# adaLN block with sliding-window attention and a gated spatial MLP: a second norm written as seven blocks of 64, its modulation in 64-row products, and a new order of all queues

## The chip, the cores and the metric

The kernel runs on one core of a Trainium2 chip. The core has five engines, each with its own queue of instructions that it works in order: TensorE (PE, matrix products; PEld is its loading of weights), VectorE (DVE), ScalarE (ACT), GpSimd (POOL) and SyncE (SP), which here only issues DMA transfers. The metric is the time of one execution on the device in microseconds; each kernel is run several times and the median is compared.

## What is computed

The input x has 2048 rows (tokens) of 448 columns. A row c of 448 gives, through silu and a product with w_mod, six rows of 448 (sa, ca, ga, sb, cb, gb). Everything is bfloat16.

```python
mod = (silu(c) @ w_mod).reshape(6, 448)          # sa, ca, ga, sb, cb, gb
h = layernorm(x) * (1 + ca) + sa
x = x + ga * attention(h, wqkv, wo)               # 16 heads of 28, causal, window of 256 rows
h = layernorm(x) * (1 + cb) + sb
z = gelu(h @ w_in)                                # 2 x 896 columns
z1, z2 = z[:, :896], layernorm(z[:, 896:])
g = w_sp @ z2 + b_sp                              # 2048 x 2048: mixes the rows
out = x + gb * ((z1 * g) @ w_out)
```

## The kernel before

**Stages.** x is held as 16 tiles of 128 rows. (1) To some 27 us: loads, the first modulation (sa, ca), the first norm and Q, K, V of the first block of four tiles. While nothing else can run, TensorE works filler products (L564). (2) To some 110 us: attention, tile by tile (scores L925, L955 and L966, exponential on ACT L911, mask on DVE L974, probabilities times V L1002, output product L1028), with Q, K and V of the next blocks of 512 rows in between (L762, L796, L820, L840). (3) To some 155 us: the gMLP's input products (L1122 for z2, L1143 for z1). (4) To some 261 us: the spatial mixing, 28 groups of 16 products (L1167), each followed by an addition on DVE (L1171) and a product on POOL (L1174). (5) Between and behind these, the output products (L1186), the last addition (L1196) and the stores.

**What sets the order.** The program creates some 1,175 operations, numbered as they are created, with the engines that each may run on and the operations that it depends on. A long string, PLAN, then has one word for each: a letter for the engine (p PE, a ACT, d DVE, t POOL, s SP), the operation's number, and the buffer slots it takes. The words stand in one global order; each engine works its own words in that order, and the waits on semaphores follow from the dependences. Priorities and costs that are also written in the code are not read when PLAN is there. So an engine can be held by a word whose input is late, and all its later words wait behind it.

**The loads.** SyncE issues, in the plan of before and in this order: x of tiles 0 and 1 (L408), two halves of wmodA, half of wk (L404), x of tiles 2 and 3, half of wq, x of tiles 4 to 7 (L398), x of 8 to 11, wv, wmodB (L393; the columns of w_mod for ga, sb, cb, gb, 1,568 KB), the four transposes of the first norm of tiles 4 to 7 (L465, from xn to hT), x of tiles 12 to 15, wo, and then transposes of later tiles among five loads of w_in (L432, L434). ACT issues c and the other halves of wmodA, wk and wq; its silu of c stands behind them.

**w_in** is 448 x 1792 and lies in four chunks of the 128 partitions: three of 128 rows, and one of the last 64 rows, which is loaded twice, once into each half of the partitions. This is so because the products L1122 and L1143 are made in pairs of 64 rows each: one uses partitions 0 to 63, the other 64 to 127, and the two of a pair belong to different outputs. by_halves (L1091) says which 64-row chunk of which output goes with which: chunks 0 to 5 are the halves of the three full chunks, and chunk 6 is the doubled one.

**The norm** (L635) computes (x - mean) * rstd into xn, on DVE (L643) or as x * rstd + (-mean * rstd) on POOL or DVE (L650). For the second norm, 448 columns are written as they are, and a second instruction (L655, L656) copies the last 64 of them again behind, so that after the transpose the last 64 rows of hT stand in both halves of the partitions. That is 16 copies of 128 x 64.

**The second modulation** (sb, cb) has to lie in the same layout. mod_cols (L526) makes it as 32 products with 112 x 128 weights from wmodB. For the last 64 columns, doubled, it takes wmodE, which two copies (twice, L581) fill from wmodB. mod_out (L553, L554) copies the result to modT. The rows ga and gb are made by 8 products of L593, from wmodB too.

Of the kernel before, what the change touches and what calls it, by code (L numbers as in the profile page):

```python
# [5 lines left out]
BF16 = mybir.dt.bfloat16  # L6
# [6 lines left out]
d24 d22 p50.1 p59.3 p51.2 p58.0 p60.1 p62.0 a0 a3 a5 a7 a9 d23 d25 d26 d27 p40.1 p68.2 p74.3 p64.1 p52.0 p67.2  # L13
p53.3 p76.0 p49.3 p70.0 s1 s2 s4 d113 s6 s10 s8 a41 p45.0 p46 p47.1 p48 p73.2 p75.1 p63.2 t30 t31 t32 t35 t36
t33 d111 d114 t34 d112 t115 t37 a103 t29 t105 t38 d117.3 d116.2 p125.7 d86 d85 p128.0 p78.0 a129 a130 d106
d126 d127 d120 d121 d118 d119 a107 p83.1 p80.0 p81.1 p79.2 p77.0 p55.3 p72.2 p71.0 s12 d183 d181 p65.1 t104
p54.0 p149.1 p84.2 p140.5 p141 p150 a151 p82.1 p57.2 a142 t109 t110 t108 p137.7 p138 a139 p66.2 t122 d124.2
d123.0 p134.3 p131.6 p69.3 p56.0 p146.0 p147 p61.2 a132 d177 d184 d135 a136 s13 d243 d179 d178 d182 d180 t28
t185 t191 t187 t189 d245 d44 d241 d186.3 s11 p143.7 p370.0 a133 p164.1 p171.6 p172 d244 p165 d166 a148 p152.0
p144 d145 d173 d247 p153 d154 a371.0 p376.0 p155.1 p156 d157 a42 a377.4 p394.0 a395.1 a396 a170 t39 d380 d372  # L20
d246 d167 d374 p158.7 p159 a160 s15 p93.1 p94 d95 d248 d87 d88 d242 d397 p96.0 p97 d98 d378 s193 t188.1 s194
t190.2 s195 t192.0 s196 d197 d200 p401.0 a402.5 p174.1 p175 a176 p161.7 p162 p373.0 p89.0 p90 d91 d198 d92
a403 a43 p421.0 a422.6.0 t249 t253 d404 t251 t199 p375 p379 p381 d406 d382 d399 t252.2 d163 p217.0 p218 a219
a169 p210.1 p211 d212 p429.0 a430.0 p201.0 p202 a203 d168 p204.1 p205 a206 s14 d309 d383.2 p398.0 p400 p448.0
a449.2.1 s16 d426 s831 s258 t254.1 s259 d250.0 d255 d425 d432 d311 s384 s257 t256.3 s260 t100 t99 t261 t102
t262 t264 p226.0 p423.0 a424 p207.1 p227 p405 p208 d228 d305 p407 d408 d409.1 d306 s410 d101 d310 d431 a209
# [224 lines left out]
def bass_adaLN_cond__sliding_block__mixer_gmlp__prompt_kernel(  # L251
# [16 lines left out]
    DC = 4  # L268
# [366 lines left out]
    def norm(slot, t, to, h, deps, prio, share, twice=False):  # L635
# [17 lines left out]
        if not twice:  # L653
            return op
# [614 lines left out]
```

## Time and profile before

| | us |
|---|---|
| runs of the kernel | 277.11, 276.43, 281.8; median 277.11 |
| the profiled execution | 277.96 |
| its span in the profile | 276.2 |
| granted clock of TensorE, mean | 0.993 |
| TensorE busy | 268.5 |
| DVE, ACT, POOL busy | 163.7, 121.5, 118.1 |

The profile is that of one execution. Its page gives the busy time of each engine, the span in 40 slices, the DMA queues, the chain of work that ended last, and groups of instructions by source line. Other views of the same trace give single instructions with what they waited for, the chain in order of time, and stretches of time with each engine's busy time. Matmuls are pipelined, so an instruction's length on PE (say 0.35 us) is longer than the distance to the next one.

### The profile page before, as it was taken

To read this page: it belongs to the slowest core of one execution; us is meant where nothing else is said; L and a number is where in the kernel's file an instruction comes from. 1 tells how busy PE (TensorE), PEld (TensorE's weight loads), DVE (VectorE), ACT (ScalarE), POOL (GpSimd) and SP (SyncE) were. 2 spreads that over 40 slices of the span, in tenths; PEclk is the share of its full clock that TensorE was granted. 3 is DMA by queue.
4 is the path that set the end of the run, shared out by engine and by line. 5 is a ranking of instruction groups with operands and counts; after the bars stand their busy time and mean duration, and the time that the engine had idled before them with its cause. 6 is when DMAs were issued, how large, how long until landed. Compare 5 with 4: busy or idle time off the path is not lost.

```text
span 276.2 us, 8403 instructions
## 1 busy us (share of the span) xinstructions
PE 268.5 (97%) x3751; PEld 155.1 (56%) x3751; DVE 163.7 (59%) x365; ACT 121.5 (44%) x142; POOL 118.1 (43%) x160
## 2 busy tenths in 40 slices
PE   7999998999999899999999999999999999999995
PEld 5976686678677676544444444444444444454552
DVE  3799999979899989939789301221212022153143
ACT  2599998899899689476766500000000000000000
POOL 7565467626574231498258003254453023062320
PEclk9999999999999799999999999999999999999999
DMA  7999744845442533658499996000000000001013
GB/s 206 316 221 189 96 101 114 107 96 110 114 63 61 107 60 61 176 114 141 97 155 191 213 182 135 0 0 0 2 0 0 0 2 0 33 17 63 0 39 116
DMA packets 67301, 25.54 MB, mean 92 GB/s; under 512 B 58497, under 2 KB 66178, under 8 KB 67266
## 3 DMA queue, kind: packets, MB, share of 16 engines
q1 hardware_dynamic: 66304, 24.21, 43.8%
q10 hardware_dynamic: 962, 0.80, 1.1%
q8 instruction: 29, 0.48, 0.8%
q14 instruction: 6, 0.05, 0.1%
HBM read 9.01 MB, written 1.84 MB: 39 GB/s over the span
## 4 chain that ended last, share of the span: by engine, by line
PE 78%; DVE 13%; DMA 4%; POOL 1%; SPq 1%; issue 1%; DVEq 0%
PE ps L1167 35%; PE ps L1122 8%; PE ps L1143 8%; PE ps L1186 8%; PE ps L1002 5%; DVE PT L974 4%; PE ps L1028 4%; PE ps L955 3%; DMA x_sb<-in_A_x_dram 3%; PE ps L820 3%; PE ps L762 2%; DVE st_all L628 2%; PE ps L840 2%; DMA hT<-xn 2%; DVE o_sb L1018 1%
## 5 line engine op out<-in xcount | busy, mean ns | idle before, releaser
L1174 POOL TENSOR_TENSOR z1T<-tmpg,z1T 128x512 bf16<-128x512 bf16 x28 | 32.0, 1153 | 77.2 <-DVE tmpg L1171 77.2
L1171 DVE TENSOR_TENSOR tmpg<-ps,bsp_bc 128x512 bf16<-128x512 f32 x28 | 19.0, 689 | 76.0 <-PE ps L1167 64.7
L911 ACT ACTIVATE PW<-ps 128x2048 bf16<-128x2048 f32 (+1 forms) x42 | 59.9, 1451 | 6.1 <-PE ps L955 4.5
L1167 PE MATMUL ps<-wspB,z 128*128 128x512 bf16 x224 | 50.1, 379 | 0.0
L1167 PE MATMUL ps<-wspA,z 128*128 128x512 bf16 x224 | 49.5, 379 | 0.0
L632 POOL TENSOR_TENSOR rs_all<-mv_all,neghalf 128x1 f32<-128x1 f32 (+2 forms) x37 | 24.1, 672 | 34.3 <-DVE mv_all L630 34.3
L974 DVE TENSOR_TENSOR PT<-PW,mask 128x1024 bf16<-128x1024 bf16 x56 | 38.0, 702 | 0.2
L1167 PEld LDWEIGHTS ps<-wspA,z 128*128 128x128 bf16 x224 | 21.8, 98 | 26.6 <-issue 0.4
L1167 PEld LDWEIGHTS ps<-wspB,z 128*128 128x128 bf16 x224 | 21.9, 98 | 26.2
L1002 PE MATMUL ps<-Vaug,PT 128*128 128x32 bf16 x496 | 23.3, 177 | 1.4 <-DVE o_sb L1018 1.4
L1002 PEld LDWEIGHTS ps<-Vaug,PT 128*128 128x128 bf16 x496 | 21.4, 96 | 4.3 <-DVE o_sb L1018 2.2
L1122 PE MATMUL ps<-w_in,hT 64*128 64x448 bf16 x224 | 22.0, 350 | 0.0
L1186 PE MATMUL ps<-w_out_g,z1T 128*128 128x448 bf16 (+2 forms) x119 | 22.0, 342 | 0.0
L1143 PE MATMUL ps<-hT,w_in 64*128 64x512 bf16 x196 | 22.0, 376 | 0.0
L628 DVE BATCH_NORM_STATS2 st_all<-z 128x6 f32<-128x448 bf16 x32 | 18.4, 606 | 5.8 <-ACT z L1129 5.8
L628 DVE BATCH_NORM_STATS2 st_all<-x_sb 128x6 f32<-128x448 bf16 x32 | 19.4, 615 | 2.9 <-DMA x_sb<-in_A_x_dram 2.7
L1002 PE MATMUL ps<-Vaug,PW 128*128 128x32 bf16 x224 | 19.7, 177 | 0.0
L820 PE MATMUL ps<-hT,WQK 112*128 112x128 bf16 x256 | 17.9, 223 | 1.6 <-DVE KT L833 1.1
L1151 ACT ACTIVATE z1T<-ps 128x512 bf16<-128x512 f32 x28 | 14.6, 603 | 9.1 <-PE ps L1143 9.1
L1196 DVE TENSOR_TENSOR fin<-ps,x_sb 128x448 bf16<-128x448 f32 (+2 forms) x17 | 9.8, 595 | 14.7 <-PE ps L1186 9.9
L1002 PEld LDWEIGHTS ps<-Vaug,PW 128*128 128x128 bf16 x224 | 17.6, 96 | 1.1
L1129 ACT ACTIVATE z<-ps 128x896 bf16<-128x896 f32 x16 | 13.9, 913 | 7.9 <-PE ps L1122 5.4
(105 smaller groups left out, 354.1 us busy)
## 6 DMA issues: line engine op xcount, KB each, us to landing
out_dram<-fin SPq DMA_DIRECT2D x15, 112.0 KB, 1.7
wmodB<-in_w_mod_dram SPq DMA_DIRECT2D x1, 1568.0 KB, 15.0
x_sb<-in_A_x_dram SPq DMA_DIRECT2D x3, 448.0 KB, 8.0
w_in<-in_B_w_in_dram SPq DMA_DIRECT2D x3, 448.0 KB, 4.5
w_out_g<-in_B_w_out_dram SPq DMA_DIRECT2D x1, 784.0 KB, 4.7
bsp_bc<-in_B_b_sp_dram SPq DMA_DIRECT2D x1, 512.0 KB, 5.1
x_sb<-in_A_x_dram SPq DMA_DIRECT2D x2, 224.0 KB, 4.8
hT<-xn SPq DMA_TRANSPOSE x28, 3.2
```

Source lines behind the costliest of these rows:

```text
L628: st = [dve(0.62, lambda e, t=t, o=12 - 6 * (n - ci), s=s: e.bn_stats(st_all[:, slot, t, o:o + 6], s()), deps(t), prio) for ci, s in enume ...
L632: return pool(0.4 + 0.15 * len(tiles), lambda e: e.tensor_tensor(rs_all[:, slot, a:b], mv_all[:, slot, a:b, 1], neghalf[:, 0:b - a], ALU.pow),
L820: km = lambda g, kc, start, stop, h=h, t=t: lambda e: e.matmul(ps[:, h.slot[0], g * 128:(g + 1) * 128], lhsT=WQK[0:CP, kc, 16 + 4 * g:20 + ...
L911: ex = act(xdur, lambda e, out_ap=out_ap, in_ap=in_ap: e.activation(out_ap(), in_ap(), ACT.Exp, scale=SCALE), [s] + list(after), v - 8.0 + ...
L974: return lock_d(0.68, lambda e: e.tensor_tensor(cols(hp.slot[0] * 2048 + 1024 * k, [[256, 4], [128, 2], [1, 128]]), cols(at_w() + pad + at ...
L1002: fns.append(lambda e, hp=hp, hO=hO, hi=hi, bi=bi, kb=kb, hd=hd, nb=nb, a=at[hi][bi], p_of=p_of: e.matmul(ps[:, hO.slot[0], 32 * hd:32 * h ...
L1122: return lambda e, kc, p0, start, stop: e.matmul(ps[:, hs[t % 2].slot[hf], 0:D], lhsT=hT[p0:p0 + 64, kc, t * 128:(t + 1) * 128], rhs=w_in[ ...
L1143: return lambda e, kc, p0, start, stop: e.matmul(ps[:, hs[b // 2].slot[b % 2], :], lhsT=w_in[p0:p0 + 64, kc, ft * 128:(ft + 1) * 128], rhs ...
L1167: m = pe(16 * MMS, [lambda e, h=h, si=si, ft=ft, tb=tb: e.matmul(ps[:, h.slot[0], :], lhsT=z2[:, si, ft * 128:(ft + 1) * 128], rhs=(wspA i ...
L1171: a = dve(0.7, lambda e, h=h, ht=ht, tb=tb: e.tensor_tensor(tmpg[:, ht.slot[0], :], ps[:, h.slot[0], :], bsp_bc[:, tb * 512:(tb + 1) * 512 ...
L1174: u = pool(1.16, lambda e, ht=ht, ft=ft, tb=tb: e.tensor_tensor(z1T[tb][:, ft, :], tmpg[:, ht.slot[0], :], z1T[tb][:, ft, :], ALU.mult), [ ...
L1186: return [lambda e, ft=ft: e.matmul(ps[:, h.slot[0], 0:hi - lo], lhsT=z1T[t // 4][:, ft, (t % 4) * 128:(t % 4 + 1) * 128], rhs=w_out_g[:, ...
```

## The change

The change makes the layout of the second norm uniform. The 448 columns are covered by eight blocks of 64, numbered by half u (0, 1) and chunk c (0 to 3): the block starts at column 192 u + 64 c. Columns 192 to 255 are thus in two blocks, u = 0, c = 3 and u = 1, c = 0; as columns these are seven different blocks.

- The norm of the second kind reads x through a four-dimensional pattern (halves) and writes 512 columns in one instruction; the 16 copies are gone.
- w_in is loaded to match in four loads of 64 partitions and two chunks each (448 KB each, 1,792 KB in all as before) instead of five.
- The second modulation is made as 64 products with 112 x 64 weights, each for one half of the output's partitions (tile_position (0, 64 u)), straight from wmodB; wmodE and its two copies are gone.
- by_halves pairs chunk n of the lower half with chunk n or n + 1 of the upper half.
- PLAN is new, with 1,156 words. Its numbers are counted anew, too, since fewer operations are created.

The diff without PLAN:

```diff
     wmodB, _, wmodB_bytes = alloc("wmodB", [128, DC, 4 * D], BF16, at=wspA_off + NT * HS)
-    wmodE, _, wmodE_bytes = alloc("wmodE", [128, DC, 2, 128], BF16, at=wspA_off + NT * HS + wmodB_bytes)
...
-    t_win_l = [load("d_win%d" % ch, "sp", 0.46, lambda e, ch=ch: e.dma_start(w_in[:, ch, :], B_w_in[ch * 128:(ch + 1) * 128, :]), (), -46.0 + 0.1 * ch)
-               for ch in range(3)]
-    t_win_l += [load("d_winh%d" % p0, "sp", 0.4, lambda e, p0=p0: e.dma_start(w_in[p0:p0 + 64, 3, :], B_w_in[384:448, :]), (), -45.6 + 0.001 * p0)
-                for p0 in (0, 64)]
+    t_win_l = [load("d_win%d" % i, "sp", 0.46, lambda e, u=u, c=c: e.dma_start(
+        w_in[64 * u:64 * u + 64, c:c + 2, :], B_w_in[192 * u + 64 * c:192 * u + 64 * c + 128, :].rearrange("(c p) n -> p c n", p=64)), (), -46.0 + 0.1 * i)
+               for i, (u, c) in enumerate(((0, 0), (1, 0), (0, 2), (1, 2)))]
+
+    def halves(row):
+        a = row[:, 0:1]
+        return bass.AP(tensor=a.tensor, offset=a.offset, ap=[a.ap[0], [64, 4], [192, 2], [1, 64]])
...
     def mod_cols(h, vs):
-        def weights(v, kc, ch):
-            at = (v - 2) * D + 128 * ch
-            if ch < 3:
-                return wmodB[0:CP, kc, at:at + 128]
-            return wmodE[0:CP, kc, v - 3, :]
-
-        return [lambda e, v=v, kc=kc, ch=ch, col=(vi * 4 + ch) * 64: e.matmul(
-            ps[:, h.slot[0], col:col + 64], lhsT=weights(v, kc, ch), rhs=sc_sb[0:CP, kc:kc + 1].broadcast_to([CP, 64]), start=(kc == 0), stop=(kc == DC - 1))
-                for vi, v in enumerate(vs) for ch in range(4) for kc in range(DC)]
+        return [lambda e, v=v, kc=kc, ch=ch, col=(vi * 4 + ch) * 64, u=u: e.matmul(
+            ps[64 * u:64 * u + 64, h.slot[0], col:col + 64], lhsT=wmodB[0:CP, kc, (v - 2) * D + 64 * ch + 192 * u:(v - 2) * D + 64 * ch + 192 * u + 64],
+            rhs=sc_sb[0:CP, kc:kc + 1].broadcast_to([CP, 64]), start=(kc == 0), stop=(kc == DC - 1), tile_position=(0, 64 * u))
+                for vi, v in enumerate(vs) for ch in range(4) for kc in range(DC) for u in range(2)]
...
-    t_two = [twice(up) for up in range(2)]
-    t_mB = pe2(1.06, mod_cols(hB, (3, 4)), [t_wmB, t_two, t_sc], MB, [hB])
+    t_mB = pe2(1.06, mod_cols(hB, (3, 4)), [t_wmB, t_sc], MB, [hB])
...
         if twice:
-            out, at = lambda: to[:, h.slot[0], 0:D], lambda: x_sb[:, t, :]
+            out = lambda: to[:, h.slot[0], :].rearrange("p (c u k) -> p c u k", c=4, u=2)
+            at = lambda: halves(x_sb[:, t, :])
...
-        if not twice:
-            return op
-        return [op, locks(add({"dve": (0.16, lambda e: e.tensor_copy(to[:, h.slot[0], D:DP], to[:, h.slot[0], DP - 128:D])),
-                         "pool": (0.25, lambda e: e.tensor_copy(to[:, h.slot[0], D:DP], to[:, h.slot[0], DP - 128:D]))}, [op], prio))]
+        return op
...
-            low, high = ([(x, k) for k in (0, 2, 4)], [(y, k) for k in (1, 3, 5)]) if up else ([(x, k) for k in (6, 0, 2, 4)], [(y, k) for k in (6, 1, 3, 5)])
-            for n in range(len(low)):
-                for (g, k), p0 in ((low[n], 0), (high[n], 64)):
-                    fns[-1].append(lambda e, g=g, k=k, p0=p0, stop=up and n == 2: g(e, k // 2, p0, k == 6, bool(stop)))
+            for n in range(3 if up else 4):
+                for g, kc, p0 in ((x, n, 0), (y, n + up, 64)):
+                    fns[-1].append(lambda e, g=g, kc=kc, p0=p0, start=not up and n == 0, stop=up and n == 2: g(e, kc, p0, start, bool(stop)))
```

Read back into operations, the first words of SyncE in the two plans are (PLAN's numbers in brackets; the transposes' numbers agree, and 17 to 21 are the w_in loads):

```
before: x 0-1 (1), wmodA (2), wmodA (4), wk (6), x 2-3 (10), wq (8), x 4-7 (12), x 8-11 (13), wv (11), wmodB (15),
        transposes of tiles 4, 5, 6, 7 (193 to 196), x 12-15 (14), wo (16), ...
after:  w_in (18), x 0-1 (1), wo (16), w_in (17), wmodA (2), wmodA (4), wk (6), w_in (19), x 2-3 (10), x 12-15 (14),
        wq (8), x 4-7 (12), w_in (20), x 8-11 (13), wv (11), transpose of tile 4, of tile 7, wmodB (15), of tile 6, of tile 5, ...
```

ACT's first words are, in the plan of before, the load of c, its halves of wmodA, wk and wq, and then silu and a zeroing of 1 us; in the new plan they are the load of c, silu, the two halves of wmodA, the zeroing, and the halves of wk and wq. On TensorE, the first product from wmodB (L593 for ga) stands in the new plan ahead of V of the fourth tile, part of the scores of query tiles 1 and 2, the second modulation and all products of the second block of rows. Of the operations that both plans have, 65 run on another engine: 18 go from ACT to DVE, 17 from DVE to ACT, 16 from POOL to DVE, 9 from DVE to POOL, 5 from POOL to ACT.

More of the change, by code (lines that the diff above doesn't have):

```diff
@@ L12 @@
 PLAN = """
[L13 to L22, printed above, removed]
@@ L347, in bass_adaLN_cond__sliding_block__mixer_gmlp__prompt_kernel @@
     wmodB, _, wmodB_bytes = alloc("wmodB", [128, DC, 4 * D], BF16, at=wspA_off + NT * HS)
[L348 to L349 removed]
+    assert qbd_bytes + qt_bytes <= NT * HS and wmodB_bytes <= NT * HS
     PW, _, pw_bytes = alloc("PW", [128, NPW * 2 * PWH], BF16, at=z2_off)
```

119 lines of the change are left out of this document (61 added, 58 removed).

## The prediction

> **What bounds the kernel now.** I read the page first, for the busy shares and the chain that ended last.
>
> ```profile
> span 276.2 us, 8403 instructions
> PE 268.5 (97%) x3751; PEld 155.1 (56%) x3751; DVE 163.7 (59%) x365; ACT 121.5 (44%) x142; POOL 118.1 (43%) x160
> PE 78%; DVE 13%; DMA 4%; POOL 1%; SPq 1%; issue 1%; DVEq 0%
> ```
>
> TensorE is busy nearly throughout, and its sum is the same work after the change, so only its gaps can be won back. The chain of waits in order of time shows where they are (start, length, what).
>
> ```profile
> 3.91 7.49 DMA x_sb<-in_A_x_dram
> 15.49 1.02 POOL rs_all L632
> 17.68 2.10 POOL xn L650 x3
> 21.05 4.35 DMA hT<-xn
> 25.43 1.12 DVE hT L731 x2
> 27.49 1.05 PE ps L820 x16
> 40.19 1.16 issue
> 110.16 2.19 PE ps L1122 x22
> ```
>
> Up to 27.49 us the end hangs on one thread: the load of x for tiles 4 to 7 (landed at 11.40), their norms, their four transposes (first issue 17.10, below; last 21.05, landed 25.40) and hT's modulation, which releases the first product of the second row block. From there the rest is mostly one queue of TensorE work. A delay of this release is therefore a delay of the end, unless gaps after it take it up. The order of issue on SyncE, and the release and a later gap on TensorE (in brackets: idle before, and releaser):
>
> ```profile
> 0.79 0.46 SPq L408 DMA_DIRECT2D x_sb<-in_A_x_dram  x1
> 3.91 1.20 SPq L398 DMA_DIRECT2D x_sb<-in_A_x_dram  x2
> 6.20 2.23 SPq L393 DMA_DIRECT2D wmodB<-in_w_mod_dram  x1
> 17.10 6.13 SPq L465 DMA_TRANSPOSE hT<-xn  x4
> ...
> 44.61 0.60 SPq L434 DMA_DIRECT2D w_in<-in_B_w_in_dram  x1
> ...
> 87.82 0.58 SPq L432 DMA_DIRECT2D w_in<-in_B_w_in_dram  x1
> ```
>
> ```profile
> 21.43 1.67 PE L593 MATMUL ps<-wmodB,sc_rep 112*128 112x448 bf16 x8
> 25.00 0.53 PE L535 MATMUL ps<-sc_sb,wmodB 112*128 112x64 bf16 x12
> 26.08 0.61 PE L955 MATMUL ps<-qT,KT 32*128 32x128 bf16 x48
> 27.49 1.05 PE L820 MATMUL ps<-hT,WQK 112*128 112x128 bf16 x16 [0.40 <-DVE modT L554]
> ```
>
> ```profile
> 90.94 0.19 PE L1002 MATMUL ps<-Vaug,PT 128*128 128x32 bf16 x1 [1.39 <-DVE o_sb L1018]
> ```
>
> The five w_in loads come between 44.61 and 87.82, when nothing waits for them. wmodB is issued at 6.20, ahead of the transposes. What the transfers carry, and how fast, stand in the page's DMA part (KB each, us from issue to landing) and in the windows (length; busy and count by engine; clock; DMA share; GB/s):
>
> ```profile
> wmodB<-in_w_mod_dram SPq DMA_DIRECT2D x1, 1568.0 KB, 15.0
> x_sb<-in_A_x_dram SPq DMA_DIRECT2D x3, 448.0 KB, 8.0
> w_in<-in_B_w_in_dram SPq DMA_DIRECT2D x3, 448.0 KB, 4.5
> wo_g<-in_A_wo_dram SPq DMA_DIRECT2D x1, 392.0 KB, 5.7
> ```
>
> The landings of x in the first 20 us (the tile's own view):
>
> ```profile
> DMA to landing us min/median/max: 2.8/7.1/8.5
> ```
>
> ```profile
> 3.60:10.30 6.70, 6.20 (x66) 4.99 (x65) 4.26 (x12) 2.78 (x6) 4.48 (x11) 1.00 1.09 302
> 10.30:14.40 4.10, 4.10 (x70) 3.92 (x68) 3.87 (x11) 2.71 (x6) 1.54 (x4) 1.00 1.11 326
> 14.40:18.00 3.60, 3.60 (x57) 2.85 (x55) 3.12 (x11) 3.57 (x6) 2.40 (x6) 1.00 1.02 284
> 91.00:96.00 5.00, 5.00 (x120) 4.01 (x120) 4.66 (x11) 2.83 (x3) 0.24 (x1) 0.66 0.54 85
> ```
>
> wmodB lands at 6.20 + 15.0 = 21.2, and L593 starts at 21.43. From 3.6 us to there the DMA engines are full (share 1.0 and over): bytes put ahead of a load delay it by their time at about 300 GB/s.
>
> **The change: SyncE's order.** By the new word list, in word order, SyncE issues w_in (second quarter), x of tiles 0 and 1, wo, w_in (first), two halves of wmodA, wk, w_in (third), x of tiles 2 and 3, x of tiles 12 to 15, wq, x of tiles 4 to 7, w_in (fourth), x of 8 to 11, wv, the transposes of tiles 4 and 7, and only then wmodB, then the transposes of 6 and 5. Ahead of x of tiles 4 to 7 stand, newly, three quarters of w_in, wo and x of 12 to 15: 3 x 448 + 392 + 448 = 2,184 KB, or 2.24 MB. At 326 GB/s that is 6.9 us, at 302 it is 7.4, at 284 (the window of wmodB's long rows, which w_in's resemble) 7.9. I take 7.3: x lands at 18.7 instead of 11.40.
>
> From x to the first transpose takes 17.10 - 11.40 = 5.7 us; the work in it (statistics on DVE, the power on POOL, the norms) is the same, so 24.4. The four issues lie (21.05 - 17.10)/3 = 1.3 us apart, so wmodB's issue, queued behind two, comes at 27.0 instead of 6.20. A load on idle DMA engines needs 2.1 us before its bytes flow (estimate: x's fastest landing above, the first 224 KB, took 2.8 us, and 0.23 MB at 302 is 0.75 of them). Its 1.61 MB take 4.9 us at 326, 5.3 at 302 and 5.7 at 284. So wmodB lands near 34.5, 13.3 us later than now.
>
> **What waits for it.** TensorE works its list in order. In the new list the first half of L593 stands ahead of the last V tile, of scores of query tiles 1 and 2, of the second modulation (L535) and of all of the second row block. So TensorE stops there until 34.5, with everything for the first block done: now that work ends before 21.43, and with wmodA, wk and wq some 4 to 7 us later it ends at about 28. Six idle us are the result. After L593 today's list needs 27.49 - 21.43 = 6.1 us to the first product of the second block. The other path, the two transposes behind wmodB, needs half of the 4.2 us by which the four now land after it (25.40 - 21.2), plus 27.49 - 25.43 = 2.1: 4.2 us. I take 5.5, TensorE's words that I count behind L593 at their present lengths: 40.0 instead of 27.49, **+12.5 us**.
>
> Idling has a second price. Today's longest gap, 1.39 us ahead of 90.94, is followed by a granted clock of 0.66 over 91 to 96: 0.34 x 5 = 1.7 us lost. A longer gap costs up to that; I take 1.0, as the first us behind it are partly covered by the transposes' path.
>
> **What can come back.** The gaps behind the release: 0.40 at 27.49, 1.16 at 40.19, 1.39 and the 1.7 of clock at 90.94, 4.65 in all. The third row block's and fourth's loads and transposes are ahead of time in the new order, and by the words 65 instructions move between engines, mostly in exchange between ACT and DVE; new gaps are as likely as the old ones to go. I take half, **-2.3**; bounds 0 and -4.65.
>
> **The other edits.** Rows by line (count | busy, mean ns), and one stretch of TensorE's L545:
>
> ```profile
> L643 DVE TENSOR_SCALAR xn<-x_sb,mv_all,rs_all 128x448 bf16<-128x448 bf16 x11 | 4.2, 394 | 0.8 <-POOL rs_all L632 0.8
> L1053 DVE TENSOR_SCALAR hT<-hT,modT 128x512 bf16<-128x512 bf16 x4 | 2.0, 507 | 0.0
> L656 POOL COPY xn<-xn 128x64 bf16<-128x64 bf16 x13 | 4.7, 367 | 2.9 <-DVE xn L643 2.7
> L655 DVE COPY xn<-xn 128x64 bf16<-128x64 bf16 x3 | 1.3, 444 | 0.0
> L582 DVE COPY wmodE<-wmodB 112x512 bf16<-112x512 bf16 x2 | 0.4, 256 | 0.0
> L545 PE MATMUL ps<-sc_sb,wmodA 112*112 112x112 bf16 x32 | 2.5, 246 | 0.4 <-DMA wmodA<-in_w_mod_dram 0.2
> ```
>
> ```profile
> 6.91 1.03 PE L545 MATMUL ps<-sc_sb,wmodA 112*112 112x112 bf16 x16 [0.21 <-DMA wmodA<-in_w_mod_dram]
> ```
>
> The copies that go are 13 x 0.367 on POOL and 3 x 0.444 + 2 x 0.256 on DVE: 6.6 us of engine time. None is a row of the chain above, and TensorE runs without a break behind them; what they could give is inside the 4.65. The norm writes 512 columns in place of 448: between nothing (one instruction as before) and 507 - 394 = 0.11 us on each of 16, beside TensorE; off the path, at nothing. Its four-dimensional pattern has no row here; the first norm's four blocks of 112 share the L643 row at the same mean, so I expect no jump. The pairs in the gMLP's products keep count and shape, 0. One w_in load fewer saves an issue of 0.6 us on SyncE, 0.
>
> The modulation turns 32 products with 128 weight columns into 64 with 64 columns. Now 12 take 0.53, (0.53 - 0.19)/11 = 0.031 apart, about 1.1 us for all 32 (25.00 to 26.08). Bounds: L955's row, (0.61 - 0.2)/47 = 0.009 apart, gives 64 x 0.009 = 0.6, a gain of 0.5; L545's 16 in 1.03, (1.03 - 0.246)/15 = 0.052 apart, give 3.4, a loss of 2.3. I take the present pace for each, 2.0, so +0.9, and it is inside the 5.5 above.
>
> **The sum.** The profiled execution took 277.96 us (span 276.2), 0.85 over the median of 277.11. 277.96 + 12.5 + 1.0 - 2.3 = 289.2; with the 0.85 taken off, **288.3 us**. Low end of this case: 326 GB/s (x at 18.3), 4.8 instead of 5.7 to the transposes (three norms at DVE's 0.394 instead of POOL's 2.10/3), wmodB 25.7 + 2.1 + 4.9 = 32.7, 4.2 behind it: 36.9, +9.4, with all 4.65 regained 281.9. High end: 284 GB/s (19.3), wmodB 27.6 + 2.1 + 6.0 (the transposes share the queue) = 35.7, then 6.1 and 2 of slow modulation: 43.8, +16.3, nothing regained, 1.7 of clock: 295.1.
>
> **The rivals.**
> 1. The delay stays small and is made up later. The stretch from 15.49 to 19.79, POOL's, takes 4.3 us; statistics of tiles 12 to 15 are done by the time x lands, so DVE could write the three norms (3 x 0.394 for 2.10) and the small steps close up, and the transposes follow x by 3.5 us and not 5.7. With 326 GB/s: x 18.3, transposes 21.8, wmodB 24.4 + 7.0 = 31.4, second block 35.6, +8.1; all 4.65 regained gives 277.1 + 8.1 - 4.65 = 280.6, within 2%. For it: the middle loses the w_in loads of 44 to 88 us and 16 copies. Against it: it needs the good end of every term, and TensorE's list is in order, so nothing is drawn forward into the gap. 0.13.
> 2. The other side: the new first loads are not waited for. If DMA engines shared their time so that x's 448 KB and wmodB's rows finished as early as now, the release would stay at 27.49 and the 4.65 would come back, at most: 277.1 - 4.65 + 0.9 of modulation = 273.4. It decides if x lands before about 12 us. Against it: in the trace loads land in the order of issue, and share 1.0 leaves no free engine; and wmodB is behind transposes that cannot be issued before x lands. 0.05; to be over 2% faster it would have to give 5.5 us, more than the gaps hold: 0.02.
> 3. The same delay, with a slow modulation: L545's pace, the 3.4 us above, 2.3 more than now, on TensorE between L593 and the second block, so 1.4 over my sum: 289.7. For it: weights of fewer than 128 columns load slowly in this trace:
>
> ```profile
> L545 PEld LDWEIGHTS ps<-sc_sb,wmodA 112*112 112x112 bf16 x32 | 2.3, 161 | 0.9 <-ACT sc_sb L518 0.6 <-DMA wmodA<-in_w_mod_dram 0.3
> L535 PEld LDWEIGHTS ps<-sc_sb,wmodB 112*128 112x128 bf16 x24 | 0.9, 97 | 0.0
> ```
>
> 161 ns against 97. The Trainium skill, TensorEngine Tiling (Array Packing), section Restrictions, says that column tiling disables fast weight load, which speaks against the 64-column products here; this trace holds the 112-column form only, and agrees so far. Against: the 64-column pairs go to separate halves of the array and may overlap. 0.20.
>
> **How the numbers follow.** My forecast has 0.62 beside these: 288 us. A measurement of this kernel can tell about 2%, 5.5 us, from no change: within 271.6 to 282.6. Faster 0.02; same 0.13 + 0.03 of rival 2 + 0.01 of the forecast's low end = 0.17; slower 0.81. The range of 8 in 10 leaves out rivals 1 and 2 and the last tip: 281 to 295.
>
> **What would show it.** In the changed profile: x of tiles 4 to 7 landing at 18 to 19 us; wmodB issued at 26 to 28 and landing at 33 to 36; a TensorE gap of 4 to 8 us, ended by wmodB, right before L593; the first L820 of the second block at 37 to 43; a half clock right behind the gap; the start of the gMLP's first products (L1122 now 110.16) at 120 to 123; and 16 x L643 and L650 with 512 columns at under 0.11 us more. I am wrong if loads do not land in order of issue, if x lands before 15, or if L1122 starts before 115.

## The result and the profile after

| | median us | range | against the kernel before, same chip |
|---|---|---|---|
| kernel before | 278.0 | 276.4 to 281.8 (4 runs) | |
| changed kernel | 295.62 | 294.36 to 296.65 (4 runs) | 1.065, 95% interval 1.057 to 1.073 |

The change makes the kernel 17 to 18 us slower. The ratios here and below compare fast executions alone (the 281.8 of the kernel before is a slow one), so they differ a little from the ratios of the medians. The direction and the mechanism of the start are as forecast; the size is above the forecast of 288 us and just outside its range of 281 to 295. The profiled execution of the changed kernel took 295.28 us, with a span of 293.5. Lines of the changed code have other numbers: L582 is the old L593, L541 the old L545, L530 the old L535, L749 the old L762, L807 the old L820, L1015 the old L1028.

The page of the changed kernel (span, busy time, granted clock of TensorE in 40 slices, chain by engine):

```profile
span 293.5 us, 8448 instructions
PE 271.6 (93%) x3773; PEld 156.1 (53%) x3783; DVE 164.7 (56%) x368; ACT 125.4 (43%) x146; POOL 104.1 (35%) x135
PEclk9999869999999999999999999999999999999999
PE 73%; DVE 12%; DMA 9%; SPq 2%; issue 1%; POOL 1%; DVEq 0%; POOLq 0%
```

TensorE's sum is nearly the same (271.6 for 268.5), and the span is 17.3 longer: the time went into gaps. The chain of waits in order of time shows the same thread as before, with longer pieces:

```profile
7.85 13.19 DMA x_sb<-in_A_x_dram
28.82 8.35 DMA wmodB<-in_w_mod_dram
37.31 0.91 PE ps L582 x2
44.67 0.43 PE ps L749 x2
123.82 4.84 DMA hT<-o_sb
```

x of tiles 4 to 7 lands at 7.85 + 13.19 = 21.04 us (before 11.40), wmodB at 28.82 + 8.35 = 37.17 (before 21.2). The DMA-issuing queue of SyncE, and TensorE's waits (in brackets), show how they are tied:

```profile
7.85 2.88 SPq L396 DMA_DIRECT2D x_sb<-in_A_x_dram  x1
...
26.17 2.61 SPq L466 DMA_TRANSPOSE hT<-xn  x2
28.82 0.58 SPq L391 DMA_DIRECT2D wmodB<-in_w_mod_dram  x1
```

```profile
12.75 1.74 PE L541 MATMUL ps<-sc_sb,wmodA 112*112 112x112 bf16 x16 [6.61 <-DMA wmodA<-in_w_mod_dram]
25.43 0.93 PE L827 MATMUL ps<-wv,hT 112*128 112x448 bf16 x4 [1.38 <-DMA wv<-in_A_wqkv_dram]
37.31 0.91 PE L582 MATMUL ps<-wmodB,sc_rep 112*128 112x448 bf16 x2 [5.47 <-DMA wmodB<-in_w_mod_dram]
...
128.71 0.93 PE L1015 MATMUL ps<-wo_g,hT 112*128 112x448 bf16 x4 [1.49 <-DMA hT<-o_sb]
```

wmodB is issued 2.65 us after the first transpose, TensorE stands for 5.47 us at L582 until it lands, and everything of the second block comes behind. A new gap of 1.49 stands at the end of the attention. The windows over these stretches (length; busy and count by engine; clock; DMA share; GB/s):

```profile
3.60:10.30 6.70, 2.54 (x12) 1.50 (x10) 2.51 (x6) 1.05 (x1) 2.55 (x8) 1.00 1.08 251
10.30:14.40 4.10, 1.65 (x17) 1.65 (x18) 0.00 (x0) 0.00 (x0) 0.00 (x0) 1.00 1.12 303
14.40:18.00 3.60, 3.60 (x32) 3.41 (x31) 1.05 (x6) 0.58 (x1) 0.56 (x1) 1.00 1.06 272
28.80:37.20 8.40, 3.04 (x58) 2.39 (x55) 3.24 (x11) 4.38 (x7) 0.01 (x1) 0.88 0.97 231
37.20:45.10 7.90, 7.79 (x151) 3.94 (x152) 4.64 (x15) 4.11 (x5) 2.50 (x3) 0.70 0.06 13
```

Before, the first window carried 302 GB/s, now 251. Behind the gap at L582 the granted clock is 0.70 for 7.9 us. The 1.00 of the first three rows says nothing, though: the trace's record of the clock begins at 18.08 us, and where there is none the view prints 1.00. Behind the gap of 6.61 us at L541 the matmuls take 300 ns each. The same ones in the kernel before (L545) take 300 up to 6.1 us and 213 from 6.3 on, so the clock was low here too.

To place the loss, each execution's TensorE timeline is cut at three first instructions: Q of the second block (512 columns; L762 or L749), the gMLP's first product, and the first product of the spatial mixing.

| profiled execution | first Q at | Q to gMLP | gMLP to mixing | mixing to end | span |
|---|---|---|---|---|---|
| before | 28.38 | 81.71 | 44.98 | 121.16 | 276.23 |
| changed | 44.51 | 81.02 | 46.97 | 121.02 | 293.52 |

Of 17.3 us, 16.1 are lost by the first cut; the attention gives 0.7 back, and 2.0 are lost at its end. The experiments below are read by the same cuts (all from profiles of one execution; the times are medians, and where there was a single run that run). On the chips of these runs the kernel before had medians of 277.35 to 278.2.

### The profile page after: what moved, and what is told of

Its sections match the earlier page's. It is cut to its first block, busy times and chain, and to the rows that moved or that the text cites. A ratio compares the mean times of both kernels' runs of the same rounds, so it can differ in the third digit from the quotient of the medians.

```text
span 293.5 us, 8448 instructions
## 1 busy us (share of the span) xinstructions
PE 271.6 (93%) x3773; PEld 156.1 (53%) x3783; DVE 164.7 (56%) x368; ACT 125.4 (43%) x146; POOL 104.1 (35%) x135
## 4 chain that ended last, share of the span: by engine, by line
PE 73%; DVE 12%; DMA 9%; SPq 2%; issue 1%; POOL 1%; DVEq 0%; POOLq 0%
PE ps L1153 33%; PE ps L1129 7%; PE ps L1172 7%; PE ps L1108 7%; DVE PT L961 5%; DMA x_sb<-in_A_x_dram 4%; PE ps L989 4%; DMA wmodB<-in_w_mod_dram 3%; PE ps L749 3%; PE ps L942 3%; PE ps L827 2%; PE ps L807 2%; PE ps L1015 2%; DMA hT<-o_sb 2%; DVE st_all L617 1%
## 5 line engine op out<-in xcount | busy, mean ns | idle before, releaser
L1160 POOL TENSOR_TENSOR z1T<-tmpg,z1T 128x512 bf16<-128x512 bf16 x28 | 32.0, 1152 | 81.7 <-DVE tmpg L1157 81.7
L1153 PE MATMUL ps<-wspB,z 128*128 128x512 bf16 x219 | 49.4, 379 | 0.3
L1153 PE MATMUL ps<-wspA,z 128*128 128x512 bf16 x219 | 48.7, 379 | 0.4 <-issue 0.2
L621 POOL TENSOR_TENSOR rs_all<-mv_all,neghalf 128x1 f32<-128x1 f32 (+2 forms) x37 | 23.5, 646 | 61.8 <-DVE mv_all L619 61.7
L961 DVE TENSOR_TENSOR PT<-PW,mask 128x1024 bf16<-128x1024 bf16 x56 | 37.4, 699 | 0.8 <-ACT PW L898 0.8
L1153 PEld LDWEIGHTS ps<-wspB,z 128*128 128x128 bf16 x224 | 21.9, 98 | 26.1
L989 PE MATMUL ps<-Vaug,PT 128*128 128x32 bf16 x496 | 25.2, 177 | 1.0 <-DVE PT L961 0.6
L989 PEld LDWEIGHTS ps<-Vaug,PT 128*128 128x128 bf16 x496 | 22.6, 96 | 6.0 <-DVE PT L961 2.4
L1108 PE MATMUL ps<-w_in,hT 64*128 64x448 bf16 x224 | 22.7, 349 | 0.0
L1172 PE MATMUL ps<-w_out_g,z1T 128*128 128x448 bf16 (+2 forms) x119 | 22.7, 342 | 0.0
L1182 DVE TENSOR_TENSOR fin<-ps,x_sb 128x448 bf16<-128x448 f32 (+2 forms) x17 | 9.8, 593 | 20.4 <-PE ps L1172 18.7
L617 DVE BATCH_NORM_STATS2 st_all<-z 128x6 f32<-128x448 bf16 x32 | 18.5, 604 | 4.5 <-ACT z L1115 4.3
L989 PE MATMUL ps<-Vaug,PW 128*128 128x32 bf16 x224 | 20.8, 176 | 0.0
L827 PE MATMUL ps<-wv,hT 112*128 112x448 bf16 x64 | 17.0, 366 | 1.4 <-DMA wv<-in_A_wqkv_dram 1.4
L807 PE MATMUL ps<-hT,WQK 112*128 112x128 bf16 x256 | 18.0, 219 | 0.2 <-DVE KT L820 0.2
```

What stands on the lines that cost most here:

```text
L617: st = [dve(0.62, lambda e, t=t, o=12 - 6 * (n - ci), s=s: e.bn_stats(st_all[:, slot, t, o:o + 6], s()), deps(t), prio) for ci, s in enume ...
L621: return pool(0.4 + 0.15 * len(tiles), lambda e: e.tensor_tensor(rs_all[:, slot, a:b], mv_all[:, slot, a:b, 1], neghalf[:, 0:b - a], ALU.pow),
L807: km = lambda g, kc, start, stop, h=h, t=t: lambda e: e.matmul(ps[:, h.slot[0], g * 128:(g + 1) * 128], lhsT=WQK[0:CP, kc, 16 + 4 * g:20 + ...
L827: m = pe2(4 * MMD, [lambda e, h=h, t=t, kc=kc: e.matmul(ps[:, h.slot[0], 0:D], lhsT=hT[0:CP, kc, t * 128:(t + 1) * 128], rhs=wv[0:CP, kc, ...
L961: return lock_d(0.68, lambda e: e.tensor_tensor(cols(hp.slot[0] * 2048 + 1024 * k, [[256, 4], [128, 2], [1, 128]]), cols(at_w() + pad + at ...
L989: fns.append(lambda e, hp=hp, hO=hO, hi=hi, bi=bi, kb=kb, hd=hd, nb=nb, a=at[hi][bi], p_of=p_of: e.matmul(ps[:, hO.slot[0], 32 * hd:32 * h ...
```

## The experiments

**The parts of the load order, taken alone.** Two runs start from the changed kernel and three from the kernel before. What moves is one word or a few of SyncE's. In the changed kernel's numbers s190 to s193 are the transposes of tiles 4 to 7, and s17 to s20 the w_in loads.

wmodB ahead of the transposes, in the changed kernel:

```diff
-... s13 ... s11 ... s190 ... s193 s15
+... s13 ... s11 s15 ... s190 ... s193
```

> The changed kernel with one word moved: wmodB is issued right behind wv, ahead of the transposes, and all other loads stay in the new order. My theory: wmodB's place behind two transposes is a part of the loss by itself. x of tiles 4 to 7 still lands at about 21 us, wmodB lands behind wv at about 30 instead of 37, the transposes land behind it at about 32, and the first product of the second block starts at 36 to 38 instead of 45: about 287 us. Rival: only the sum of bytes ahead of the second block counts, and these are the same: 293 us or more.

Measured: 290.68 us (one run). x still lands at 20.4, wmodB at 31.6 instead of 37.2, first Q at 36.86. The start fell by 7.7 us, within the theory's 7 to 9. The end did not follow all the way, and the time is above the expected 287: gMLP to mixing took 49.5 us, 2.5 more than in the changed kernel. wmodB's place is a cost by itself.

w_in behind the second block's transposes, in the changed kernel:

```diff
-s18 ... s1 s16 s17 ... s19 s10 ... s20 ... s192 s191
+... s1 s16 ... s10 ... s192 s191 s18 s17 s19 s20
```

> The changed kernel with its four w_in loads moved behind the four transposes of the second block; wmodB stays behind two transposes. My theory: 1,344 KB less stand ahead of x of tiles 4 to 7 and 1,792 KB less ahead of wmodB; at 251 to 303 GB/s, as the changed kernel's windows show, x lands at 15 to 16 us instead of 21 and everything behind it moves by 5 to 7 us: 288 to 291 us. Rival: the loads in halves of the partitions disturb less than counted and the order of issue is what counts: 293 us or more.

Measured: 291.36 us (one run). x lands at 14.0, wmodB at 31.7, first Q at 38.52, 6.0 us earlier than in the changed kernel, inside the theory's 5 to 7; the time is just over the expected 288 to 291. In the attention 2 us went again, in a gap that is explained below.

The kernel before with the new order of SyncE's loads, w_in in its old form:

```diff
-s1 s2 s4 s6 s10 s8 s12 s13 s11 s15 s193 s194 s195 s196 s14 s16 ... s21 s17 ... s18 ... s19
+s18 s1 s16 s17 s2 s4 s6 s19 s10 s14 s8 s12 s20 s21 s13 s11 s193 s194 s15 s195 s196
```

> The kernel before, its five w_in loads, wo, x of tiles 12 to 15 and wmodB moved to the places that the new order gives them; nothing else changed, so the layout of the norm and all other queues are those of before. My theory: the order of the loads alone makes the loss: x of tiles 4 to 7 lands at 18 to 21 us, wmodB at 34 to 37, 290 to 296 us. Rival: the other queues (ACT's loads behind silu, TensorE's order) or the new layout carry half of it: 286 us or less.

Measured: 295.64 us (one run), the changed kernel's own time. First Q is at 46.89; TensorE waits:

```profile
12.66 3.21 PE L542 MATMUL ps<-sc_sb,wmodA 112*112 112x112 bf16 x32 [7.60 <-DMA wmodA<-in_w_mod_dram]
25.99 0.55 PE L837 MATMUL ps<-wv,hT 112*128 112x448 bf16 x2 [1.74 <-DMA wv<-in_A_wqkv_dram]
38.31 3.17 PE L590 MATMUL ps<-wmodB,sc_rep 112*128 112x448 bf16 x8 [5.76 <-DMA wmodB<-in_w_mod_dram]
```

These are the changed kernel's three waits. So the order of the loads is sufficient for the loss: with the old layout and all other queues of before, it makes 18.5 us by the first cut in this one execution.

Its halves, in the kernel before: the five w_in loads early, and wmodB behind two transposes.

```diff
-s1 s2 s4 s6 s10 s8 s12 ... s15 ... s193 s194
+s18 s17 s1 s2 s4 s6 s19 s10 s8 s12 s20 s21 ... s15 ... s193 s194
```

> The kernel before with its five w_in loads alone at the places of the new order; wo, x of tiles 12 to 15 and wmodB stay. My theory of bytes ahead: 1,344 KB ahead of x of tiles 4 to 7, 1,792 ahead of wmodB; at 251 to 303 GB/s x lands at 16 to 17, wmodB at 27 to 28.5, the second block's first Q product at 34 to 36 instead of 28.4: 282.5 to 286 us. Rival: the new order's loss is wmodB's place and not the bytes: 280 us or less.

Measured: 287.5 us (one run), first Q at 39.10. x lands at 19.0 and not at 16 to 17: 1.38 MB cost 7.6 us here, 181 GB/s by that sum, though the windows of this run carry 230 to 286 GB/s. The packets explain the difference: up to the landing of x this run moved 4.62 MB (243 GB/s over 19.0 us), the kernel before 2.85 MB (250 GB/s over 11.40 us). That is 1.77 MB more, so some 0.4 MB of loads issued behind x had moved before x was complete.

```diff
-s15 ... s193 ... s194
+... s193 ... s194 s15
```

> The kernel before with wmodB alone moved behind the first two transposes of the second block; all other loads stay. My theory: x of tiles 4 to 7 lands at 11.4 as before, the transposes are issued at 17.1, wmodB at 19.7, landing 7 to 8.3 us later at 27 to 28 instead of 21.2; the second block's first Q product at 34 to 35 instead of 28.4: 282 to 285 us. Rival: TensorE's other work covers it: 280 us or less.

Measured: 288.63 us (one run), first Q at 39.88. x lands at 10.8 as before, wmodB is issued at 20.59 and lands only 10 us later, at 30.6, and TensorE stands for the longest time of all the runs:

```profile
20.59 1.28 SPq L390 DMA_DIRECT2D wmodB<-in_w_mod_dram  x1
```

```profile
30.68 3.17 PE L590 MATMUL ps<-wmodB,sc_rep 112*128 112x448 bf16 x8 [8.28 <-DMA wmodB<-in_w_mod_dram]
```

Each half costs 10.7 to 11.5 us at the first cut, well over what was expected; together with wo and x of tiles 12 to 15 they make 18.5 and not their sum. A wait for wmodB that covers the others would explain that; it was not taken apart.

**Undoing the loads.** All of SyncE's loads back in the old order, in the changed kernel (wmodB behind wv; x of 12 to 15, wo and w_in behind the transposes of the second block):

```diff
-s18 ... s1 s16 s17 ... s2 s4 s6 ... s19 s10 ... s14 s8 ... s12 ... s20 ... s13 ... s11 ... s190 ... s193 s15 ... s192 s191
+... s1 ... s2 s4 s6 ... s10 ... s8 ... s12 ... s13 ... s11 s15 ... s190 ... s193 ... s192 s191 s14 s16 s18 s17 s19 s20
```

> The changed kernel with SyncE's loads back in the order of before (wmodB ahead of the transposes; x of tiles 12 to 15, wo and the four w_in loads behind them); ACT's, TensorE's, DVE's and POOL's new orders and the new layout stay. My theory: the loss is gone: x of tiles 4 to 7 lands at 11 to 12.5 us, the second block starts at 27 to 30, 276 to 281 us. Rival: the other new orders cost by themselves (ACT issues its halves of the weights behind silu, new gaps in the attention): 284 us or more.

Measured: 292.11 us, ratio 1.049 (1.039 to 1.058). The theory failed in this form: wmodB lands at 21.9, near the 21.2 of the kernel before, and yet first Q is at 39.98. The chain and TensorE's timeline of this run tell why:

```profile
25.54 3.71 DMA x_sb<-in_A_x_dram
29.28 1.15 DVE st_all L614 x2
```

```profile
32.01 0.93 PE L579 MATMUL ps<-wmodB,sc_rep 112*128 112x448 bf16 x2 [8.06 <-DVE qT L786]
```

The new list of DVE has the statistics of tiles 12 to 15 ahead of sc_rep, the other operand of L579, and of Q's copies. With this x issued late again, DVE stood still, and TensorE behind it. The new lists are made for the early loads; taking these back alone moves the wait to another engine. So x of tiles 12 to 15 was put ahead of wmodB:

```diff
-s11 s15 ... s192 s191 s14 s16
+s11 s14 s15 ... s192 s191 s16
```

> As the run with the loads back, but x of tiles 12 to 15 is issued behind wv and ahead of wmodB. In that run DVE, whose new list has the statistics of tiles 12 to 15 ahead of the copy that L593's weights need, waited for this x to 29.3 us, and TensorE behind it for 8.2 us. My theory: that wait took the place of the one removed. Now x of 12 to 15 lands at about 16 to 17, wmodB at 22 to 24, the first product of Q for the second block (28.4 in the kernel before, 40.0 with the loads back) starts at 30 to 33: 279 to 284 us. Rival: the loss of the first 40 us has another cause, the first product stays at 36 or later: 287 us or more.

Measured: 290.27 us (one run). First Q is at 31.41, as expected, so the first 40 us are explained. But the time is 290 and not 279 to 284: Q to gMLP took 88.24 us instead of 81. It begins with this, in the chain:

```profile
34.48 0.04 PE ps L986 x2
34.52 3.52 issue
38.04 0.24 PE ps L986 x2
```

"issue" names no wait. At that time wo and four w_in loads, 2.2 MB, were on the way (issued 26.0 to 29.3, landed 30.9 to 40.1). The next run puts w_in later, among the transposes:

```diff
-s191 s16 s18 s17 s19 s20 ... s432 ... s320 ... s509
+s191 s16 ... s432 s18 s17 ... s320 s19 s509 s20
```

> As the last run with the loads back and x of tiles 12 to 15 early (290.3 us), but the four w_in loads stand one or two at a time among later transposes, as in the kernel before, and not all behind the second block's. In that run TensorE stood for 3.5 us at 34.5 with no wait that the profile names, while 2.2 MB of wo and w_in were on their way. My theory: the burst made that gap and the slow clock behind it; without it the stretch from the first Q product to the gMLP falls from 88.2 to 81 to 82.5 us: 281.5 to 284 us. Rival: the gap has another cause in the new order and stays: 287 us or more.

Measured: 287.01 us (one run). The gap went from 34.5 but came back, 3.06 us long, at 69.93, just behind the w_in loads at their new place (issued 56.2 to 63.0, landed 61.8 to 70.0): Q to gMLP 87.70. The stretch did not shorten, so the expected time failed; that the gap moved with the loads speaks for the theory. With ACT's order and w_out's place undone as well:

```diff
-a0 ... a40 a3 ... a5 a41 ... a7 a9
+a0 ... a3 ... a5 ... a7 a9 a40 a41
...
-s366 s741
+s741 s366
```

> As the run with w_in spread, and two more steps undone: ACT issues its halves of wmodA, wk and wq ahead of silu again, and the load of w_out stands behind the transpose of attention's tile 14. My theory: ACT's order gives 1 to 2.5 us at the start (first Q product at 29 to 30.5) and w_out's place the 1.5 to 2 us that TensorE waits at the end of the attention: 278 to 281 us. Rival: neither counts: 281.5 us or more.

Measured: 287.61 us, ratio 1.036 (1.032 to 1.040). First Q is at 28.42: the start is that of the kernel before, to 0.04 us, and ACT's order was worth 1.7 (30.12 before it). The gap stands in TensorE's timeline, followed by a low clock in the windows:

```profile
71.28 0.26 PE L939 MATMUL ps<-qT,KT 32*32 32x96 bf16 x10 [2.99 <-issue]
```

```profile
60.00:68.00 8.00, 7.74 (x214) 5.49 (x210) 7.10 (x16) 6.92 (x8) 3.68 (x4) 1.00 1.20 189
68.00:76.00 8.00, 5.01 (x157) 4.39 (x142) 3.58 (x10) 3.05 (x4) 4.73 (x9) 0.79 0.27 52
```

At the end nothing was gained: gMLP to mixing was 48.22, 1.8 more than the 46.42 before these two steps, and the time as a whole is not shorter. w_out's place was tried alone too, in the changed kernel, with the same move of s366:

> The changed kernel with the load of w_out alone moved behind the transpose of attention's tile 14. In the changed kernel this transpose lands 4.9 us after its issue at 123.8, with w_out's 784 KB ahead of it, and TensorE waits 1.5 us for it. My theory: the transpose lands after 2.5 to 3 us, the wait is gone, and the stretch from the gMLP's first product to the mixing falls from 47.0 to 45 to 45.6 us: 293.5 to 294.5 us. Rival: other transposes are behind which it queues anyway: 295 us or more and a stretch of 46.5 or more.

Measured: 297.65 us, ratio 1.071 (1.068 to 1.075), gMLP to mixing 48.61. It is no remedy: the wait of L1015 is gone, but others take its place (1.2 and 1.3 us for DVE), and the stretch is longer than the 46.97 of the changed kernel.

**The gaps without a named wait.** In the kernel before, the five w_in loads in one burst behind the second block's transposes and wo:

```diff
-s14 s16 ... s21 s17 ... s20 ... s18 ... s19
+s14 s16 s17 s18 s19 s20 s21
```

> The kernel before with its five w_in loads moved together behind the second block's transposes and wo, where they start at about 24.5 us. Theory A: 1,792 KB on the way at once delay TensorE's 16 KB packets of instructions, which come about every 4.2 us: between 28 and 42 us one gap of 1.5 to 4 us without a named wait, ending 1.3 to 1.5 us after a packet's landing: 279 to 284 us. Theory B: the packets pass the loads, no such gap over 1 us, the time stays at 276 to 278.5 us.

Measured: 279.7 us (one run). The kernel before ran from 276.6 to 280.3 us on this chip, so the time alone shows nothing. TensorE's timeline has one gap of this kind over 1 us, and it ends as expected:

```profile
38.46 0.29 PE L817 MATMUL ps<-hT,WQK 112*128 112x128 bf16 x2 [1.71 <-issue]
```

The trace holds packets of 16 KB on a queue that it calls "instruction". They come some 4 to 5 us apart in the attention, and are late in these five runs:

```
run (moved in it)              packet before  late packet     its      gap of       gap ends after
                               starts         starts          landing  TensorE      the landing
w_in late                      22.23          40.55           41.91    41.56-43.26  1.35
loads back, x 12-15 early      26.43          35.27           36.64    34.52-38.04  1.40
w_in spread                    63.64          70.59           71.62    69.93-72.99  1.37
ACT, w_out back                61.91          68.90           69.93    68.29-71.28  1.35
before, w_in in one burst      30.36          36.03           37.10    36.75-38.46  1.36
```

In the first run the packets lie far apart also because TensorE stood for wmodB in between. In all five the gap ends 1.35 to 1.40 us behind a packet's landing. In the last three the late packet starts 0.6 to 1.2 us after the last w_in load has landed (69.96, 68.26 and 34.80), as it would if it had stood behind them.

The trace doesn't name the engine that the packets are for, but their spacing does. In the kernel before, TensorE starts on average 254 matmuls and weight loads between one packet and the next in the attention, where the packets come 4.6 us apart, and 251 to 256 in the mixing, where they come 26 to 28 us apart. The packets follow TensorE's count of instructions and not the time, so they are TensorE's.

The profiled execution of the new layout alone (next part) has two more such gaps:

```profile
78.63 1.61 issue
97.77 1.27 issue
```

They end 1.45 and 1.41 us behind a packet's landing, and there a single w_in load was on the way or had just landed (71.00 to 77.54, and 92.83 to 98.50). A burst is therefore not needed.

The form of the w_in loads as a cause: the kernel before with four loads into half of the partitions, at the same places.

```diff
-w_in[:, ch, :], B_w_in[ch * 128:(ch + 1) * 128, :]
+w_in[64 * u:64 * u + 64, c:c + 2, :], rows 128 * c + 64 * u + p and the same of the next chunk
```

> The kernel before with its w_in loads alone in the form of the change: four loads of 64 partitions and two chunks, same layout in memory as before, at the same places of the list (the fifth place is left out); nothing else changed. Theory A: the form of these loads is what costs the new layout its 1% in the old order: they take 5 to 6.5 us to land instead of 3.3 to 4.8, delay TensorE's instruction packets, and gaps of TensorE without a named wait of over 1 us appear at 55 to 100 us: 279.5 to 282 us. Theory B: the form doesn't count, the norm of 512 columns or the chance spread of the runs does: within 0.5% of the kernel before and no such gap.

Measured: 278.1 us, ratio 1.000 (0.993 to 1.006). At these late places the form shows no cost. Last, the loads of w_in one by one, with ACT's order back and w_out at its new place:

```diff
-... s381 s406 ... s816 s319 ... s432 s318 ... s809 s484
+... s381 s18 s406 ... s816 s17 s319 ... s432 s19 s318 ... s809 s20 s484
```

> The changed kernel's layout and queues, with SyncE's loads back, x of tiles 12 to 15 ahead of wmodB, ACT's order back, w_out at its new place, and the four w_in loads at four places some 10 us and more apart (about 40, 52, 70 and 85 us). Theory A (loads together delay TensorE's instructions): the gap of 3 us and the slow clock behind it go, the stretch from the first Q product to the gMLP is 81.5 to 83.5 instead of 86.9, and the stretch behind it 46 to 47.5: 278.5 to 281.5 us. Theory B: the new order loses there for other reasons: 284 us or more.

Measured: 282.82 us, ratio 1.017 (1.008 to 1.025); the profiled execution took 281.3. Q to gMLP is 83.27, so 3.7 of the 5.2 us went with the spreading, and no gap without a wait over 0.6 us is left. The time lies between the two theories' ranges. The w_in loads came 7 to 8 us apart (40.3 to 63.3), less than I meant. What is left against the kernel before is 1.6 in the attention and 1.9 at its end.

**The new layout alone.** The changed program with the old list of words:

> The new layout alone: the changed program with the kernel before's whole word list, renumbered, without the words of the removed copies and of the fifth w_in load. My theory: the layout costs and gives nearly nothing: 64 products of the second modulation in 1.0 to 1.3 us instead of 1.08, norms of 512 columns 0.1 to 0.2 us longer on DVE and POOL but off TensorE's path, copies off the path: 275.5 to 278.5 us, within 0.5% of the kernel before. Rival: the four-dimensional pattern or w_in's loads into half of the partitions cost more: 280 us or more; or the copies held something: 275 or less.

Measured: 281.1 us, ratio 1.010 (1.006 to 1.013). The theory's 275.5 to 278.5 failed, and the time is in the rival's range: the layout gives nothing, and costs about 1% with the old lists. The one execution that was profiled took 284.8 us, longer than the median, so the 1% cannot be read off it. The form of w_in in the old layout doesn't make it (above); the second modulation isn't it either: in the run with ACT's order back its 64 products take the time from 25.1 to 26.1.

```profile
L527 PEld LDWEIGHTS ps<-sc_sb,wmodB x64: 106/111/113, 25.1 to 26.1; 112*64 112x64 bf16 x64
L527 PE MATMUL ps<-sc_sb,wmodB x64: 193/193/217, 25.1 to 26.1; 112*64 112x64 bf16 x64
```

What remains is the norm of 512 columns, the lists, which are not fitted to it, and gaps like the two above; that was not taken apart.

**The price of the idle clock.** 48 filler products in the gap of the changed kernel, whose results nothing reads:

```diff
-... a157 p90.1
+... a157 p1156.1 p90.1      # 48 products of fill with fill, 128 x 256
```

> The changed kernel with 48 filler products (128 x 256, nothing reads them) on TensorE right ahead of the first product that waits for wmodB; they fall into the gap of 5.5 us. My theory: the granted clock of 0.70 over 37 to 45 us comes from the gap and costs (1 - 0.70) x 7.9 = 2.4 us; with the gap filled the clock there is 0.95 or more and the time falls by 1.5 to 2.5 us, to about 293.5. Rival: the stretch behind the gap is bound by the transposes' path and not by TensorE's clock: the time stays within 0.7 us of the changed kernel's 295.6.

Measured: 297.22 us, ratio 1.069 (1.062 to 1.076), beside 1.065 for the changed kernel: no gain. The windows say that the clock did stay:

```profile
36.00:41.00 5.00, 4.83 (x45) 4.10 (x43) 0.71 (x3) 1.28 (x3) 0.00 (x0) 1.00 1.22 218
41.00:46.00 5.00, 5.00 (x146) 2.95 (x147) 3.71 (x13) 3.29 (x5) 1.94 (x3) 1.00 0.07 13
```

From wmodB's landing to first Q the stretch fell from 44.51 - 37.17 = 7.3 to 46.00 - 40.9 = 5.1 us, the 2.2 that a clock of 0.70 costs. But in this execution x landed at 24.0 and wmodB at 40.9, 3 to 4 us later than in the changed kernel, and Q to gMLP took 1.5 longer. The loads were behind well before the fillers start, so how much of that is theirs stays open; what the clock is worth in the whole is not settled.

## Where the prediction held, and which of its steps failed

Right: SyncE's loads land in their order of issue, wmodB's place behind the transposes holds TensorE's list at L582 (the old L593), a low clock follows, and what is lost at the start arrives at the end. The gap there is 5.5 us and I said six, but that is partly luck: both of its ends were late, the work before it ended at 31.84 and not at 28, and wmodB landed at 37.17 and not at 34.5. The rival that the loads are not waited for fell with x's landing at 21.04. The slow modulation fell too, and with it my own +0.9 for it: the 64-column products start some 16 ns apart, and 64 of them take the 1.0 us that 32 took before. Their weight loads are slow, 111 ns for half the columns against 97, but the products start that close together all the same, so it costs no time here. The Trainium skill says that column tiling disables fast weight load (TensorEngine Tiling (Array Packing), Restrictions); the 111 ns agree with that. My row for it, 161 ns for 112 columns, was misread: it is a mean over a slow start, with a median of 132 and a longest load of 214. And the old trace held a second form of fewer than 128 columns, L955's weights of 32 columns, which load in 88 ns.

The sum of the prediction was 289.2 for a profiled execution; it was 295.28. The 6.1 us lie in these steps:

- **x of tiles 4 to 7 lands at 18.7: it was 21.04.** The step "2.24 MB at 302 GB/s" is off by 2.3 us. The bytes were right: 5.11 MB moved before the landing (243 GB/s over 21.04 us), 2.26 more than before. The rate was not: the first window carried 251 GB/s and not 302, and the 3.6 us before it 76 and not 115. The rate of the old mix of loads was taken for the new one. In the first window the fall goes with w_in in its new form: the four executions with these loads first carried 251 to 259 GB/s there, the run with w_in late 306, and the two runs of the kernel before with w_in first in its old form 298 and 288. In the first of these two x still landed only at 20.49; 5.4 MB had moved by then.
- **5.7 us to the first transpose: it was 5.1**, 0.6 gained.
- **wmodB lands 7.5 us after its issue: it was 8.35**, 0.9 lost. The window carried 231 GB/s and not 302; transposes were on the same queue, but how much of the loss is theirs is not shown. The run with wmodB alone behind shows how far this can go, 10 us.
- **5.5 + 1.0 us to the first product of the second block: it was 7.3**, 0.8 lost. The clock of 0.70 over 7.9 us is 2.4 us of TensorE, more than the 1.7 that I set as the most; I took 1.0 because the transposes' path would cover the rest. The run with fillers took 5.1 from landing to Q, near my 5.5 without the clock.
- **-2.3 us regained: it was +0.3** (span +17.3, first product of the second block 27.49 to 44.51, +17.0). Some gaps did go: from the first product of the second block to the gMLP it is 82.6 us before and 81.0 now. But 2.0 us were lost at the end of the attention, among them the 1.49 in which L1015 waits for a transpose. A new wait there was in the prediction only as "new gaps are as likely". Every run with the new lists has it, in size 1.4 to 4.5; runs with the old ones never over 0.3. w_out's place isn't its cause, and which word is stays open.

The first four make 3.5, the last 2.6; the two large steps that failed are the rate of the first loads and the half of the old gaps that was to come back. Two readings of the other edits were off as well; whether they show in the time was not tested: a norm of 512 columns takes 0.16 us longer than one of 448 on DVE (597 against 441 ns, L633) and 0.19 on POOL (1029 against 844, L640), where I set under 0.11; and one of the copies that went did stand in the old chain (0.59 us of L655 at 81.81).

One thing was not in the prediction at all: with the new lists, Q to gMLP is 81.0 to 82.5 us when w_in, wo and x are loaded first, and 83.0 to 88.2 us when w_in's loads ran in the attention. The old lists bore w_in there in the kernel before (81.7, and 80.5 with w_in in halves), though not in one burst (84.1), nor in the profiled execution of the new layout (87.1). So the early loads buy something, but less than they cost. No version that I ran is faster than the kernel before: the best with the new layout has 281.1.

## What to carry to other kernels

In a fixed order of queues, a load is priced by what stands behind it: count the bytes ahead of the first load that an engine needs, then look for loads that are issued behind an instruction which itself waits. Take the GB/s of a mix of loads that resembles the new one, and keep the lower end: in two of these runs 0.3 to 0.4 MB more than the loads ahead of x had moved before x was complete. Undoing one queue of a planned order is no clean experiment, because the other queues are fitted to it; put the suspected part into the old kernel as well.

## What the runs showed of the hardware

Large loads can delay TensorE without any wait that the profile names. Its instructions come in packets of 16 KB, one for some 250 matmuls and weight loads (254 in the attention and 251 to 256 in the mixing of the kernel before). When loads of 0.5 to 2.2 MB were on the way or had just landed, a packet came late and TensorE stood until 1.35 to 1.45 us after its landing: five gaps of 1.7 to 3.5 us, and two of 1.3 and 1.6. In the kernel before, 1.8 MB in one burst made one of 1.71 that the other order of the same loads does not have.

A low granted clock follows some gaps of TensorE and not others, and the length of the gap alone does not decide it. It was 0.66 over 5 us behind 1.39 us of idling in the kernel before, and 0.70 over 7.9 us behind 5.47 in the changed kernel. It was 1.00 behind the 1.49 us at L1015 of the changed kernel, and behind the 1.70 of the run with w_in late. Where the record of the clock has not begun, the lengths of like matmuls tell it: 300 ns in the changed kernel's first modulation against 213 in that of before.

A load of 1.6 MB took 15.0 us when issued early among others, 8.35 when issued behind two transposes, and 10 when two more transposes and two more loads came right behind it: the time from issue to landing tells little without its neighbours.
